# Attention and a gated long convolution: the fourth and fifth batch's last pair turned on TensorE, the last outputs reordered, and the order planned anew

## The chip, the cores and the metric

The kernel runs on one core of one Trainium2 chip. The metric is device time in microseconds (us). The kernel before took 386.67 us, the median of five runs (385.62 to 388.58).

A core has five engines that run side by side and wait for each other through semaphores: TensorE (PE: matrix products, and transposes against an identity matrix), ScalarE (ACT), VectorE (DVE), GpSimd (POOL) and SyncE (SP, which here only issues DMAs). Each engine works through its own list of instructions in order. TensorE writes to PSUM, which has eight banks. The rest lies in SBUF.

## The reference

There are 8 batches, 12 heads, 448 positions and 64 numbers per head. The first half is an attention with one extra term in the denominator; the second half projects its output three ways, convolves one of them cyclically along the sequence by means of a Fourier transform, multiplies the three and projects again.

```python
def _attn_ref(q, k, v):
    scale = 1.0 / np.sqrt(q.shape[-1])
    scores = scale * np.matmul(q, k.transpose(0, 1, 3, 2))
    m = np.max(scores, axis=-1, keepdims=True)
    e = np.exp(scores - m)
    attn = e / (np.sum(e, axis=-1, keepdims=True) + np.exp(-m) + 1e-09)
    return np.matmul(attn, v)

def _moe_ref(x, w_proj, filter_fft, w_out):      # x: (8, 448, 768), the heads side by side
    proj = x @ w_proj                            # w_proj: 768 x 2304
    x1, x2, x3 = proj[..., :D], proj[..., D:2 * D], proj[..., 2 * D:]
    X2 = np.fft.rfft(x2, n=S, axis=1)
    H = np.fft.rfft(filter_fft, n=S, axis=0)[None, :, :]
    x2_conv = np.fft.irfft(X2 * H, n=S, axis=1)
    return (x1 * x2_conv * x3) @ w_out
```

The kernel leaves out the subtraction of the maximum: dividing `exp(scores)` by its sum plus one is the same quotient.

## The kernel before

**Attention.** The heads go in pairs, six pairs to a batch, 48 in all (pair `i` belongs to batch `i // 6`; this document counts batches "first" to "eighth" in words, and from 0 in the code). For a pair, TensorE forms the scores (lines 773 and 775), ScalarE takes their exponential out of PSUM (780 and 786), TensorE multiplies them with v (798 and 806; the last column of v is one and gives the sum), and VectorE divides (819 to 821). The result lies in a tile `xb`, with positions down the partitions.

**From `xb` to `xT`.** The second half needs x with its 768 columns down the partitions, so each pair's `xb` is transposed into a tile `xT`. There are two ways. `x_dma` (line 892) lets SP issue one transposing DMA for several pairs; it is issued once after pair 2 of a batch, for pairs 0 to 2, and once for the rest. `x_pe` (line 901) makes four transposes on TensorE into a PSUM bank, and `x_back` copies them out (line 910 on VectorE, 908 on ScalarE). The first two batches use TensorE for all their pairs. The third batch uses DMA for pairs 0 to 4 and TensorE for pair 5. Which batches give pair 5 to the second DMA too is the constant `XALL`: before, the fourth to the eighth.

```python
if b in XALL or b > 1 and hp < NHP - 1:
    if hp in (2, NHP - 1 if b in XALL else NHP - 2):
        ps = range(0, 3) if hp == 2 else range(3, hp + 1)
```

**The second half**, `dense(b)`. VectorE folds `xT` (950 to 958). TensorE projects the fold, in the first four batches by blocks of frequencies (`P`, line 981), in the last four by columns (`PT`, line 1011), where the result, `x2T`, is turned by two transposing DMAs from SP (`rows_back`, line 1028). It is transformed (`Z`, 1049; copied by ScalarE at 1057), multiplied with the filter's spectrum (VectorE, 1063 and 1069), and transformed back (`I`, 1134, copied out at 1143, unfolded by VectorE at 1152 to 1163). The two other projections are the gates `G` (line 1095, six matmuls each, one for each of the six column blocks of `xT`); ScalarE copies the first (1107), VectorE multiplies it with the second (1110), and the product with the convolution at 1178. The output projection is `O` (line 1207): `st` 0 to 2 are the first three blocks of 128 positions, `st` 3 is the last 64 positions of two batches at once; each has two halves of 384 columns. ScalarE copies a half to a tile `osb` (1219, three buffers), and SP stores the 768 columns when both halves are there (1226, and 1229 for `st` 3).

**The last rows.** For the eighth batch the outputs came in the order `st` 0, 1, 3, 2, and `st` 2 had its own function `O_last` (line 1261 ff.): three pieces of 384, 192 and 192 columns, copied by ScalarE, ScalarE and VectorE into the free tile `nat` and stored by SP, ScalarE and SP, each as soon as it is copied.

**Loads.** In the first two batches q, k and v are cast and q and k turned on TensorE. From the third on, q comes by a casting load that GpSimd issues (536), k and v by SP's loads (585) that GpSimd casts (590 and 602), and q and k are turned by transposing DMAs from SP (542 and 547). The weights come by GpSimd's loads: `w_proj` in parts (751), the filter (667 ff.) and `w_out` (756).

**Who decides the order.** Every piece of work is a task with an engine, a planned cost, a due time, what it needs and makes, and which PSUM bank or buffer it takes and gives back. `Plan.run` runs through time on these costs: each engine that is free takes the ready task that is due first. The result is each engine's list of instructions; on the chip nothing is reordered. Due times come from the constants at the head of the kernel (`ATT`, `SLOT`, `DENSE`, `PACE`, `LEAD`, `LOAD` and others). For a DMA the planner adds 1.8 us and the task's own `late` to the transfer. PSUM banks are handed out by the same plan.

Of the kernel before, what the change touches and what calls it, by code (L numbers as in the profile page):

```python
# [19 lines left out]
D = H * DH  # L20
SP = 112
NST = S // SP
NDT = D // 128
NHP = H // 2
SCALE = 1.0 / float(np.sqrt(DH))
DCH = 384
# [15 lines left out]
class Plan:  # L42
# [26 lines left out]
    def add(self, eng, cost, want, emit, need=(), make=(), take=(), give=(), dma=0.0, run=256, n=1, after=0.0, begun=(), late=0.0):  # L69
        self.tasks.append((want, len(self.tasks), eng, cost, emit, need, make, take, give, dma, after, run, n, begun, late))  # L70
# [186 lines left out]
def kernel(  # L257
# [11 lines left out]
    nc = tc.nc  # L269
# [1 line left out]
    MAGIC = 12582912.0  # L271
    NSTAGED = 2
    SPIN = 38
    EARLY1 = 2.19
    ATT = [0.75, 24.41, 87.21, 101.61, 150.77, 186.69, 235.26, 286.49]
    SLOT = [2.52, 8.01, 4.27, 4.82, 6.44, 0.30, 6.71, 5.19]
    DENSE = [46.81, 84.00, 123.83, 169.80, 218.58, 253.46, 313.76, 296.92]
    PACE = [2.16, 2.30, 2.04, 2.28, 1.15, 2.55, 0.60, 1.33]
    FOLD = [-0.20, 0.45, -42.13, -39.60, 2.51, 0.15, -6.85, 0.77]
    BPS = 1.67  # L280
    RE1 = 22.20
    WT = 1.31
    FT = 21.96
    HALVED = (2,)
    AHEAD = [0, 0, 33.95, 43.62, 34, 34, 34, 34]
    LEAD = [-14.87, 8.62, 5.03, 10.66]
    LOADS = ((1, 0), (1, 1), ("F", None), (0, None), (2, None), ("O", None))
    LOAD = [22.29, 18.40, 18.46, 37.27, 38.16, 45.94]
    STEP = 2.26
    BYCOL = (4, 5, 6, 7)  # L290
    GLAST = 40.00
    XALL = (3, 4, 5, 6, 7)
    FOLD0 = (52.22, 39.65, 43.44)

    const = ctx.enter_context(tc.tile_pool(name="const", bufs=1))
    wts = ctx.enter_context(tc.tile_pool(name="wts", bufs=1))
# [16 lines left out]
    wout_bf = wts.tile([128, NDT, D], BF16, name="wout_bf")  # L313
# [8 lines left out]
    kT = [const.tile([128, NHP, 4, 128], BF16, name=f"kT{i}") for i in range(2)]  # L322
# [14 lines left out]
    nf = nat.bitcast(F32)  # L337
# [13 lines left out]
    add = plan.add  # L351
# [4 lines left out]
    def bank(hy):  # L356
        i = plan.banks[hy][0]
        return psum[:, 512 * i : 512 * i + 512]
# [167 lines left out]
    def loaded(b):  # L526
# [3 lines left out]
        parts = 2 if b in HALVED else 1  # L530
        size = NHP // parts
        few = 1 if b == NSTAGED else 3
# [20 lines left out]
        n = 0  # L553
        for part in range(parts):
            gs = slice(size * part, size * part + size)
            for st in range(NST):
                room = [("c" + w, i0 - 2) for w in "kqv"] if b == NSTAGED else [("qturn", b - 1, st)]
                add("POOL", 0.8 if parts > 1 else 0.95, want + STEP * n, lambda st=st, gs=gs: q_load(st, gs), need=room,
                    make=[("qn", b, part, st)], dma=1.3 / parts)
                n += 1  # L560
                add("SP", 1.3, want + 6.0 + STEP * n, lambda st=st, gs=gs: q_turn(st, gs), need=[("qn", b, part, st), last],
                    make=[("qturn", b, st)] + [("qT", i0 + i) for i in range(gs.start, gs.stop)], dma=0.6 / parts, late=0.7)

        for n, (name, x) in enumerate((("k", k), ("v", v))):
            add("SP", 0.5, tau(i0) - LEAD[0] - 0.2 + 0.1 * n,
                lambda name=name, x=x: nc.sync.dma_start(rests[:, "kv".index(name)], shared(x, b)),
                need=[("cr" + name, b - 1)], make=[("r" + name, b)], dma=1.05)
# [7 lines left out]
        for hp in range(NHP):  # L575
            g = i0 + hp
            for n, (name, x) in enumerate((("k", k), ("v", v))):
                slot = 2 * (g - NHP * NSTAGED) + n
                at = (KNAT + NST * D) // 2 + 384 * (slot % 5)
                src = nf[:, at : at + 384]  # L580
                old = slot - 5
                room = [("c" + "kv"[old % 2], NHP * NSTAGED + old // 2)] if old >= 0 else [
                    ("c" + w, i) for w in "kqv" for i in range(NHP * NSTAGED - 2, NHP * NSTAGED)]
                add("SP", 0.52, tau(g) - LEAD[0] + 0.1 * n,
                    lambda x=x, hp=hp, src=src: nc.sync.dma_start(src.rearrange("p (u c) -> p u c", u=2), rows(x, b, hp)),
                    need=room, make=[("s" + name, g)], dma=0.7, run=768)
                sv = src.rearrange("p (u j d) -> p u j d", u=2, j=3)
                if name == "k":
                    add("POOL", 0.6, tau(g) - LEAD[1],
                        lambda hp=hp, sv=sv: nc.gpsimd.tensor_copy(  # L590
                            kn[:, hp, 1:4].rearrange("p j (u d) -> p u j d", u=2), sv
                        ),
                        need=[("sk", g)] + (["zero kn"] if b == NSTAGED else [("kT", g - NHP)]), make=[("ck", g)])
                    if hp % few == 0:
                        gs = range(g, g + few)
                        add("SP", 1.3, tau(g) - LEAD[2], lambda hp=hp: k_turn(hp), need=[("ck", i) for i in gs] + [("crk", b), last],
                            make=[("kT", i) for i in gs], dma=0.6 * few, late=0.7)
                else:

                    def cast(hp=hp, sv=sv):  # L600
                        for u in range(2):
                            nc.gpsimd.tensor_copy(vn[b % 2][:, hp, 4 * u : 4 * u + 3, 0:DH], sv[:, u])  # L602

                    add("POOL", 0.72, tau(g) - LEAD[3], cast, need=[("sv", g), ("V", g - 2 * NHP, 1)], make=[("cv", g), ("v", g)])
# [104 lines left out]
    W = {}  # L709
# [51 lines left out]
    def attention(i):  # L761
# [153 lines left out]
        if b in XALL or b > 1 and hp < NHP - 1:  # L915
            if hp in (2, NHP - 1 if b in XALL else NHP - 2):
                ps = range(0, 3) if hp == 2 else range(3, hp + 1)
                add("SP", 1.3, w, x_dma, need=[("xb", NHP * b + h) for h in ps] + old,
                    make=[m for h in ps for m in (("X", NHP * b + h), ("xT", b, h))], dma=0.5 * len(ps), late=1.2)
        else:  # L920
            add("PE", 0.23, w, x_pe, need=[("xb", i)], make=[("X", i)], take=[("hy", ("X", i))])
            add("ACT" if on_act else "DVE", 0.43 if on_act else 0.33, w - 1.0, x_back, need=[("X", i)] + old, make=[("xT", b, hp)], give=[("hy", ("X", i))])


    def dense(b):
# [4 lines left out]
        def span(cost):  # L930

            w = DENSE[b] + at[0] * PACE[b]
            at[0] += cost
            return w
# [9 lines left out]
        def hold(key):  # L944
            return ("hy", key)
# [88 lines left out]
        def PT(dt):  # L1034
            hy = hold(("PT", b, dt))
            w = span(1.15)
            add("PE", 1.15, w, lambda: columns(dt, hy), need=[("xf", b, pg) for pg in range(4)] + [("w", 1, ch) for ch in range(2)],
                make=[("PT", b, dt)], take=[hy], give=[("xf", b)])
            add(("ACT", "DVE")[dt % 2], (0.43, 0.55)[dt % 2], w, lambda: columns_back(dt), need=[("PT", b, dt)],
                make=[("x2T", b, dt // 3)], give=[hy])  # L1040
            if dt % 3 == 2:
                ch = dt // 3
                add("SP", 1.3, w, lambda: rows_back(ch), need=[("x2T", b, ch)], make=[("x2", b, pg, ch) for pg in range(4)],
                    take=[("x2", b)], dma=1.5, late=1.2)

        def spectrum(pg, ch, hy):
            K = BLK_K[pg]
# [199 lines left out]
            if ch == 1:  # L1247
                add("SP", 0.6, w, lambda: store(st), need=[("os", b, st)], make=[("store", b, st)], give=[os_], dma=1.4, run=3072)

        def O_last(st):  # L1250
            rs = slice(st * 128, (st + 1) * 128)
            parts = ((0, DCH, "ACT"), (DCH, DCH // 2, "ACT"), (DCH + DCH // 2, DCH // 2, "DVE"))
            for n, (at, size, by) in enumerate(parts):
                hy = hold(("O", b, st, n))
                w = span(0.97 * size / DCH)
                c = slice(at, at + size)

                def product(hy=hy, c=c, size=size, n=n):
                    L["O", st, n] = bank(hy)
                    for dt in range(NDT):  # L1260
                        nc.tensor.matmul(
                            L["O", st, n][:, 0:size], W["yT", b][:, dt, rs], wout_bf[:, dt, c], start=(dt == 0), stop=(dt == NDT - 1)
                        )

                def back(size=size, c=c, n=n, by=by):
                    (nc.scalar.copy if by == "ACT" else nc.vector.tensor_copy)(nf[:, c], L["O", st, n][:, 0:size])

                def store_part(c=c, n=n):
                    (nc.scalar if n == 1 else nc.sync).dma_start(out[b, rs, c], nf[:, c])

                add("PE", 0.98 * size / DCH, w, product, need=[("y", b, 0), "wout"], make=[("O", b, st, n)], take=[hy],
                    give=[("yT", b)])
                add(by, (0.38, 0.25, 0.28)[n], w, back, need=[("O", b, st, n)], make=[("os", b, st, n)], give=[hy])
                add("ACT" if n == 1 else "SP", 0.6, w, store_part, need=[("os", b, st, n)], make=[("store", b, st, n)],
                    dma=1.4 * size / D, run=1536)

        if b and b + 1 < n_batches:
            G(0, 0), G(0, 1)
        if b in BYCOL and b + 1 == n_batches:
# [21 lines left out]
        for dt in range(NDT):  # L1301
            I(dt), G(2 + (dt + 1) // 2, (dt + 1) % 2)
        G(5, 1)
        for st in range(3) if b % 2 == 0 and b + 1 < n_batches else (0, 1, 3, 2) if b + 1 == n_batches else range(4):
            if (b, st) == (n_batches - 1, 2):
                O_last(st)
                continue
            for ch in range(2):
                O(st, ch)


    E = mybir.EngineType
# [103 lines left out]
```

## Time and profile before

| | |
|---|---|
| median of five runs | 386.67 us (385.62 to 388.58) |
| the profiled execution | 386.99 us |
| its span (first to last instruction on the core) | 384.9 us |
| TensorE, matmuls | 366.5 us, 95% of the span |
| TensorE, weight loads (beside matmuls) | 224.3 us, 58% |
| ScalarE | 261.2 us, 68% |
| VectorE | 259.2 us, 67% |
| GpSimd | 113.2 us, 29% |
| moved by DMA | 62.5 MB |

The profile is of one execution. Times in it are from the start of the span. A busy TensorE isn't TensorE at its peak: matmuls are pipelined, so the interval from one start to the next says more than the duration of one. `PEclk` is the clock that TensorE was granted, in tenths. A line of a timeline gives the start, the time, the engine, the line of the kernel, the operation, what it writes and reads and how often; the brackets at its end give how long the engine stood idle ahead of it, and for whom. `SPq` is SP's queue. In a list of waits the three numbers are the total, how often, and the longest.

### The profile page before, as it was taken

How to read it: one execution, taken by the hardware profiler on the slowest of the kernel's cores; microseconds unless marked ns; L12 is line 12 of the kernel's file. 1: busy time of each engine (PE TensorE's matmuls, PEld its weight loads, DVE VectorE, ACT ScalarE, POOL GpSimd, SP SyncE). 2: the span in 40 equal slices, each digit the busy share in tenths (PEclk: the TensorE clock that was granted, in tenths of full speed). 3: DMA queues.
4: the chain of work that ended last, by engine and by line, in shares of the span. 5: the costliest groups of instructions: out<-in, count | busy, mean ns of one | idle time of the engine just before them, and what ended most of it. 6: DMA issues, size and time to landing. Idle time of an engine off the chain costs nothing.

```text
span 384.9 us, 9526 instructions
## 1 busy us (share of the span) xinstructions
PE 366.5 (95%) x3678; PEld 224.3 (58%) x3678; DVE 259.2 (67%) x671; ACT 261.2 (68%) x456; POOL 113.2 (29%) x232
## 2 busy tenths in 40 slices
PE   8878999899999999969999999999999999999995
PEld 7546765566655676634675555555555655655553
DVE  7587579945789649647258974774369935982780
ACT  6777876666776878855688856685788757633633
POOL 5597383132464344614346350000000000000000
PEclk9999999999999999996999999999999999999999
DMA  8999999999999999999799996952241135045305
GB/s 205 242 249 242 241 211 214 133 99 281 192 215 213 129 277 233 207 162 274 182 255 158 197 254 116 176 143 84 75 93 21 22 84 122 3 84 122 125 0 165
DMA packets 149965, 62.53 MB, mean 162 GB/s; under 512 B 114525, under 2 KB 146464, under 8 KB 149920
## 3 DMA queue, kind: packets, MB, share of 16 engines
q1 hardware_dynamic: 112352, 52.05, 62.4%
q0 software_dynamic: 37184, 9.54, 26.7%
q8 instruction: 29, 0.48, 0.5%
q10 hardware_dynamic: 384, 0.33, 0.3%
q14 instruction: 16, 0.13, 0.1%
HBM read 43.86 MB, written 11.01 MB: 143 GB/s over the span
## 4 chain that ended last, share of the span: by engine, by line
PE 73%; DVE 14%; DMA 4%; issue 3%; ACT 3%; SPq 1%; POOL 1%; DVEq 0%; POOLq 0%; ACTq 0%
PE psum L1095 22%; PE psum L1207 13%; PE psum L806 8%; PE psum L981 7%; PE psum L773 7%; PE psum L1011 7%; DMA xT<-xb 2%; PE psum L1049 2%; DVE t L1063 2%; PE psum L775 2%; DVE xb L821 2%; PE psum L1134 2%; DMA nat<-in_q_dram 2%; DVE xf L958 1%; DVE cv L1163 1%
## 5 line engine op out<-in xcount | busy, mean ns | idle before, releaser
L780 ACT ACTIVATE e<-psum 128x896 bf16<-128x896 f32 x144 | 125.5, 923 | 23.2 <-PE psum L773 22.2
L1095 PE MATMUL psum<-xT,wproj_bf 128*128 128x448 bf16 x576 | 122.7, 356 | 4.6 <-DMA xT<-xb 3.5
L1095 PEld LDWEIGHTS <-wproj_bf 128*128 128x128 bf16 x576 | 54.6, 98 | 51.5 <-issue 8.8
L1207 PE MATMUL psum<-wout_bf,yT 128*128 128x384 bf16 x276 | 50.6, 326 | 0.0
L1107 ACT CAST x<-psum 128x448 bf16<-128x448 f32 x48 | 25.8, 537 | 30.0 <-PE psum L1095 23.7
L806 PE MATMUL psum<-vn,e 128*128 128x65 bf16 x1152 | 45.3, 195 | 0.0
L1219 ACT COPY osb<-psum 128x384 f32<-128x384 f32 x54 | 25.2, 483 | 23.7 <-PE psum L1207 23.3
L773 PE MATMUL psum<-qT,kT 64*128 64x448 bf16 x288 | 41.2, 358 | 0.0
L806 PEld LDWEIGHTS <-e 128*128 128x128 bf16 x1152 | 39.5, 98 | 2.6
L1063 DVE TENSOR_TENSOR t<-xs,hrs 113x768 bf16<-113x768 bf16 (+1 forms) x64 | 34.2, 573 | 8.5 <-ACT xs L1057 8.3
L602 POOL CAST vn<-nat 128x192 bf16<-128x192 f32 x72 | 27.4, 407 | 34.6 <-DMA nat<-in_v_dram 24.0
L819 DVE TENSOR_SCALAR rec<-psum 128x8 f32<-128x8 f32 x48 | 7.8, 161 | 43.6 <-PE psum L806 32.9
L1207 PEld LDWEIGHTS <-yT 128*128 128x128 bf16 x276 | 26.2, 97 | 18.3 <-issue 1.1
L1110 DVE TENSOR_TENSOR g<-x,psum 128x448 bf16<-128x448 bf16 x48 | 29.5, 616 | 9.4 <-PE psum L1095 7.3
L536 POOL DMA_DIRECT2D nat<-in_q_dram x28 | 24.8, 890 | 34.8 <-DMA qT<-nat 27.7
L981 PE MATMUL psum<-wproj_bf,xf 128*113 128x384 bf16 x192 | 35.0, 327 | 0.0
L821 DVE TENSOR_TENSOR xb<-psum,rec 128x512 bf16<-128x512 f32 x48 | 33.2, 691 | 1.7
L1011 PE MATMUL psum<-xf,wproj_bf 128*128 128x452 bf16 x144 | 30.4, 356 | 0.0
L1057 ACT CAST xs<-psum 113x384 bf16<-113x384 f32 (+1 forms) x64 | 27.5, 498 | 3.5 <-PE psum L1049 2.6
L786 ACT ACTIVATE er<-psum 128x448 bf16<-128x448 f32 x48 | 26.8, 558 | 4.5 <-PE psum L775 4.1
L1143 ACT CAST cr<-psum 128x452 bf16<-128x452 f32 x48 | 24.7, 555 | 6.4 <-PE psum L1134 6.4
L981 PEld LDWEIGHTS <-xf 128*113 128x113 bf16 x192 | 24.8, 132 | 6.8 <-issue 0.7
(117 smaller groups left out, 460.2 us busy)
## 6 DMA issues: line engine op xcount, KB each, us to landing
nat<-in_k_dram SPq DMA_DIRECT2D x48, 192.0 KB, 5.4
nat<-in_v_dram SPq DMA_DIRECT2D x48, 192.0 KB, 5.4
out_dram<-osb SPq DMA_DIRECT2D x23, 384.0 KB, 3.3
nat<-in_q_dram POOLq DMA_DIRECT2D x20, 168.0 KB, 7.9
nat<-in_q_dram SPq DMA_DIRECT2D x11, 224.0 KB, 6.8
wproj_bf<-in_moe_w_proj_dram POOLq DMA_DIRECT2D x2, 1152.0 KB, 16.6
rests<-in_k_dram SPq DMA_DIRECT2D x8, 192.0 KB, 5.3
rests<-in_v_dram SPq DMA_DIRECT2D x8, 192.0 KB, 7.0
```

Of the source, the lines that this page charges most:

```text
L602: nc.gpsimd.tensor_copy(vn[b % 2][:, hp, 4 * u : 4 * u + 3, 0:DH], sv[:, u])
L773: nc.tensor.matmul(sc[:, u, 0:S], kT[b % 2][c, hp, t, :], qT[b % 2][c, hp, :])
L780: nc.scalar.activation(e[:, 0 : 2 * S].rearrange("p (u n) -> p u n", u=2), pair(("sc", ("S", i, t)))[:, :, 0:S], AF.Exp, scale=SCALE,)
L806: nc.tensor.matmul(out_bank(u)[:, n, :], P["e"][1 + t][:, u * S + n * 128 : u * S + n * 128 + 128], vn[b % 2][:, hp, 4 * u + t, :], start= ...
L821: nc.vector.tensor_tensor(W["xb", b][:, hp].rearrange("p n (u d) -> p u n d", u=2), op[:, :, :, 0:DH], rec[:].unsqueeze(3).to_broadcast([1 ...
L981: nc.tensor.matmul(pps[:FQ, :DCH], W["xf", b][:, pg, kt, 0:FQ], wproj_bf[:, kt, D + ch * DCH : D + (ch + 1) * DCH], start=(kt == 0), stop= ...
L1011: nc.tensor.matmul(pps[:, 0 : 4 * FQ], wproj_bf[:, kt, D + dt * 128 : D + (dt + 1) * 128], W["xf", b][:, :, kt, 0:FQ], start=(kt == 0), st ...
L1057: nc.scalar.copy(L["xs", par, ch][:K, pg % 2, :], L["Z", pg, ch][:K, :DCH])
L1063: nc.vector.tensor_tensor(t[:K], L["xs", par, ch][:K], h, op=ALU.mult)
L1095: nc.tensor.matmul(p[:, :S], wproj_bf[:, kt, 2 * part * D + dt * 128 : 2 * part * D + (dt + 1) * 128], xT()[:, kt, 0:S], start=(kt == 0), ...
L1110: nc.vector.tensor_tensor(g[:, dt, :], L["x1", dt], p[:, :S], op=ALU.mult)
L1207: nc.tensor.matmul(ops[:n, :DCH], y[:, dt, 0:n], wout_bf[:, dt, ch * DCH : (ch + 1) * DCH], start=(dt == 0), stop=(dt == NDT - 1),)
```

## The change

It has three parts. `XALL` leaves out the fourth and fifth batch, so these turn pair 5 of x on TensorE as the third does, and their second transposing DMA takes pairs 3 and 4 alone. `O_last` is gone: the eighth batch's last rows go through `O` like all others, with ScalarE's copies and one store of 768 columns, and the outputs' halves come in another order. The planner is told that three kinds of transposing DMA land later (`late`), and its due times are others. The computation is the same.

```diff
-    EARLY1 = 2.19
-    ATT = [0.75, 24.41, 87.21, 101.61, 150.77, 186.69, 235.26, 286.49]
-    SLOT = [2.52, 8.01, 4.27, 4.82, 6.44, 0.30, 6.71, 5.19]
-    DENSE = [46.81, 84.00, 123.83, 169.80, 218.58, 253.46, 313.76, 296.92]
-    PACE = [2.16, 2.30, 2.04, 2.28, 1.15, 2.55, 0.60, 1.33]
-    FOLD = [-0.20, 0.45, -42.13, -39.60, 2.51, 0.15, -6.85, 0.77]
-    BPS = 1.67
-    RE1 = 22.20
+    EARLY1 = 5.03
+    ATT = [0.79, 17.21, 90.53, 105.41, 147.12, 188.78, 237.77, 285.73]
+    SLOT = [2.38, 8.68, 4.01, 3.23, 6.89, 0.31, 4.90, 5.05]
+    DENSE = [43.97, 82.34, 125.97, 170.34, 220.10, 253.73, 311.48, 304.06]
+    PACE = [1.76, 2.32, 1.55, 2.33, 1.19, 2.38, 0.76, 1.20]
+    FOLD = [-0.20, 0.39, -46.27, -39.52, 1.71, 0.19, -8.61, 0.59]
+    BPS = 1.80
+    RE1 = 13.75
...
-    FT = 21.96
+    FT = 20.85
...
-    AHEAD = [0, 0, 33.95, 43.62, 34, 34, 34, 34]
-    LEAD = [-14.87, 8.62, 5.03, 10.66]
+    AHEAD = [0, 0, 48.31, 45.28, 34, 34, 34, 34]
+    LEAD = [-24.87, 14.95, 5.88, 4.42]
...
-    LOAD = [22.29, 18.40, 18.46, 37.27, 38.16, 45.94]
-    STEP = 2.26
+    LOAD = [18.82, 18.41, 10.28, 37.96, 41.97, 46.86]
+    STEP = 1.79
...
-    XALL = (3, 4, 5, 6, 7)
-    FOLD0 = (52.22, 39.65, 43.44)
+    XALL = (5, 6, 7)
+    FOLD0 = (63.46, 45.82, 34.40)
...
                         add("SP", 1.3, tau(g) - LEAD[2], lambda hp=hp: k_turn(hp), need=[("ck", i) for i in gs] + [("crk", b), last],
-                            make=[("kT", i) for i in gs], dma=0.6 * few, late=0.7)
+                            make=[("kT", i) for i in gs], dma=0.6 * few, late=1.5)
...
                 add("SP", 1.3, w, x_dma, need=[("xb", NHP * b + h) for h in ps] + old,
-                    make=[m for h in ps for m in (("X", NHP * b + h), ("xT", b, h))], dma=0.5 * len(ps), late=1.2)
+                    make=[m for h in ps for m in (("X", NHP * b + h), ("xT", b, h))], dma=0.5 * len(ps), late=1.2 if b > 4 else 3.0)
...
                 add("SP", 1.3, w, lambda: rows_back(ch), need=[("x2T", b, ch)], make=[("x2", b, pg, ch) for pg in range(4)],
-                    take=[("x2", b)], dma=1.5, late=1.2)
+                    take=[("x2", b)], dma=1.5, late=2.5)
...
-        def O_last(st):
...
-        for st in range(3) if b % 2 == 0 and b + 1 < n_batches else (0, 1, 3, 2) if b + 1 == n_batches else range(4):
-            if (b, st) == (n_batches - 1, 2):
-                O_last(st)
-                continue
-            for ch in range(2):
+        if b + 1 == n_batches:
+            for st, ch in ((0, 0), (0, 1), (1, 0), (3, 0), (3, 1), (1, 1), (2, 0), (2, 1)):
                 O(st, ch)
+        else:
+            for st in range(3 + b % 2):
+                for ch in range(2):
+                    O(st, ch)
```

On each engine this gives another order of instructions, for the due times and the planned landings decide it.

More of the change, by code (lines that the diff above doesn't have):

```diff
@@ L1248, in O @@
                 add("SP", 0.6, w, lambda: store(st), need=[("os", b, st)], make=[("store", b, st)], give=[os_], dma=1.4, run=3072)
-        def O_last(st):
[L1251 to L1275, printed above, removed]
         if b and b + 1 < n_batches:
```

## The prediction

> **What bounds the kernel now.** I read the page first: who is busy, and where in the span TensorE is not.
>
> ```profile
> span 384.9 us, 9526 instructions
> PE 366.5 (95%) x3678; PEld 224.3 (58%) x3678; DVE 259.2 (67%) x671; ACT 261.2 (68%) x456; POOL 113.2 (29%) x232
> ...
> PE   8878999899999999969999999999999999999995
> ...
> PEclk9999999999999999996999999999999999999999
> ```
>
> TensorE is the bound: after its first 40 us it has one hole, in the slice of 173 to 183 us, where its clock falls too. TensorE's own list of waits names it:
>
> ```profile
> PE psum L901 <- DVE xb L821: 4.3, 3, 1.5
> PE psum L1095 <- DMA xT<-xb: 3.5, 1, 3.5
> ```
>
> The timelines of TensorE and of SP, and one line of the chain of waits, show the place:
>
> ```profile
> 167.70 0.35 PE L775 MATMUL psum<-qT,kT 128*128 128x448 bf16 x1
> 167.88 1.86 PE L1095 MATMUL psum<-xT,wproj_bf 128*128 128x448 bf16 x9
> 173.25 1.28 PE L1095 MATMUL psum<-xT,wproj_bf 128*128 128x448 bf16 x3 [3.50 <-DMA xT<-xb]
> 174.46 0.93 PE L773 MATMUL psum<-qT,kT 64*128 64x448 bf16 x4
> 175.18 0.43 PE L798 MATMUL psum<-vn,er 64*128 64x65 bf16 x8
> 175.54 1.50 PE L806 MATMUL psum<-vn,e 128*128 128x65 bf16 x24
> 176.85 2.43 PE L1095 MATMUL psum<-xT,wproj_bf 128*128 128x448 bf16 x6
> 179.07 0.52 PE L775 MATMUL psum<-qT,kT 128*128 128x448 bf16 x1
> 179.53 0.55 PE L773 MATMUL psum<-qT,kT 64*128 64x448 bf16 x4
> ```
>
> ```profile
> 162.69 1.58 SPq L542 DMA_TRANSPOSE qT<-nat  x1
> 164.72 4.39 SPq L892 DMA_TRANSPOSE xT<-xb  x1
> ```
>
> ```profile
> 164.72 8.48 DMA xT<-xb
> ```
>
> The gate products of the fourth batch (b = 3) have done three of six matmuls when they need x of pairs 3 to 5. That x was divided by 161.2, SP reached its transpose at 164.72, behind one of q, and it landed at 173.21. TensorE stood 3.50 us and then ran slow: 173.25 to 179.53 is 6.28 us for work that elsewhere takes 3.28 (half a gate 0.57, scores with rests 0.61, two value products 0.77, a gate 1.14, one score 0.19). The stop costs 3.50 + 3.00 = 6.5 us.
>
> **What the Trainium skill says.** "TensorE: Matmul & The Clock Gate", What's actually happening: a window of about 3.4 us without work halves TensorE's clock until it has been busy about as long. The trace agrees: 3.50 us idle, clock 0.79 over 168 to 176 us. "DMA: Bandwidth & Descriptors", Issuing engines are not separate DMA queues: transfers from SP, ScalarE and GpSimd share the same 16 engines. That fits: x transposes land in 3.3 to 10.0 us, median 3.9, the slow ones beside loads (DMA share 1.76 over 168 to 176).
>
> **The change, part by part.** I put the two programs' orders of TensorE work side by side and gave each piece its usual start-to-start time in this trace, so distances below are TensorE work.
>
> *X of the fourth and fifth batch.* The second DMA carries pairs 3 and 4 alone and starts from pair 4's value products. From there to the first gate it has 19.8 us (before 9.0, from pair 5's); in the fifth batch 18.1 (before 15.3). Pair 5 goes through TensorE: 13 us lie from its transposes to the gate. The slowest latency, 10.0, fits twice, less SP's queue. So the stop goes: -6.5. Added: eight transposes.
>
> ```profile
> L901 PE MATMUL psum<-ident_bf,xb x52: 217/219/230, 16.0 to 128.8; 128*128 128x128 bf16 x52
> ```
>
> Four start within 0.23 us (the matmul's 219 ns overlap), 2 x 0.23 = +0.46 on TensorE. The skill's Clock Gate page, Part 4: PE-mode transpose, prices one at 275 ns in context; at most 8 x 0.275 = 2.2 if nothing overlapped, and the trace decides. Two 0.38 us copies go to VectorE (67% busy), behind 13 us of other work. Each transpose stands 2.5 and 2.1 us after its pair's value products; third batch, 2.0, not stopped. SP issues as many transposes, two shorter; before the fifth batch's second stand two q transposes and four k and v loads whose buffers are free by then. Without that cover the wait is a new stop of the same kind.
>
> *The planner's times.* With transposes planned 0.8 to 1.8 us later, all is ordered anew. The first 44 us of TensorE work are the same but for neighbours swapped. The other handoffs over SP gain distance: third batch's second x 7.4 to 9.3, sixth 9.9 to 17.0, seventh 9.0 to 12.3; x2 at least 7.9 (before 6.9). The k of pairs 18 to 20 (landed 122.15, used 124.89, only 2.7 to spare) moves up: GpSimd casts pair 18's v ahead of the q load that held it for 5.1 us, so the k load that waits for that buffer goes out ahead of the x transpose and not behind, and SP reaches this k with one load fewer in between, by about 3 us. The k of pair 14 moves back behind two stores that end at 83; it landed at 87.4 and is used at 94.5, so the 2 to 3 us fit into 7. Stores that pass k and v loads cost SP 0.33 to 0.5 each, within the same distances.
>
> Second gain: at 58 us the scores of pair 9 take 1.33 instead of 0.61, a bank late from ScalarE; at 66 a gate takes 2.72 instead of 1.14, for the transpose behind it waits for `xb` 9, which stands on VectorE behind the whole fold of the second batch's first half. Now `xb` 9, pair 11's copies and pair 9's x come ahead of the fold; the transpose stands 1.6 us behind its value products and needs 0.2 + 1.05 + 0.2 plus what VectorE has left over. I leave 0.6 of the 2.3: -1.7 (0 to -2.3).
>
> Loss: some pieces move up to their bank's release: the first output of the third batch (1.57 us after the gate whose product frees the bank), a gate of the fourth, an output of the fifth (1.49), the sixth's second pair of outputs, the seventh's columns behind its fold. Each needs about 0.2 + 0.61 + 0.2 = 1.0 if VectorE is free, up to 0.8 more behind a division or product: 0 to 3, I take +0.8.
>
> *The end.*
>
> ```profile
> 378.53 2.13 PE L1261 MATMUL psum<-wout_bf,yT 128*128 128x384 bf16 x18
> ...
> 379.76 0.76 ACT L1266 COPY nat<-psum 128x384 f32<-128x384 f32 x2 [0.55 <-PE psum L1261]
> 380.44 1.12 SPq L1269 DMA_DIRECT2D out_dram<-nat  x2
> 380.55 0.37 ACTq L1269 DMA_DIRECT2D out_dram<-nat  x1
> 380.84 0.36 DVE L1266 COPY nat<-psum 128x192 f32<-128x192 f32 x1 [6.55 <-ACT nat L1266]
> ```
>
> The matmul time of the last rows is the same (0.98 against 2 x 0.49). The last copy is ScalarE's 0.48 of 384 columns for VectorE's 0.36 of 192: +0.12. The last store carries 384 KB: this trace's landed in 2.30 to 4.03 at the end, the last 96 KB in 2.66. The skill ("DMA: Bandwidth & Descriptors", Anatomy of one DMA) gives 2.0 us + bytes / 436 GB/s, so 2.9 and 2.2 by estimate, +0.7. I take 3.0 for 2.66. Its buffer is the first store's, issued 5 us before and landed in 2.3: free. +0.5 (0 to +1.6).
>
> **The sum.** -6.5 + 0.46 - 1.7 + 0.8 + 0.5 = -6.4. The profiled execution took 386.99 (span 384.93), 0.3 above the median of 386.67. 386.67 - 6.4 = 380.3 us.
>
> **Rivals.**
> *A wait comes back elsewhere* (0.14). Earlier TensorE meets the same loads sooner: pair 18's k had 2.7 us, and it is 2 us less if only TensorE moves; or one of the moved-up pieces stands behind VectorE and takes 3. 1.5 to 4.5 of the gain return: about 383. Against: that k's chain moves up as well.
> *The stop isn't typical* (0.08). It hangs on one transpose's 8.48 us; with 3.7, as in quiet stretches, it would have landed in time for none of it. Then only -1.7 + 0.46 + 0.8 + 0.5 remains: 386.7. Against: q's transpose issued beside it took 9.1, the traffic is the kernel's own, and five runs lie within 3 us.
> *VectorE becomes the bound* (0.03), in the stretches where it is 90% busy (60 to 80, 290 to 300): 385.
> *Slower: the third part of w_proj comes late* (0.05). Its load moves on GpSimd's queue behind three more casts, from 36.4 to about 41.4, where w_out's stood; its first user starts near 60. Before, the three big loads took 13.9, 19.3 and 21.2 us, but landed 7 us apart (48.5, 55.7, 62.6): they follow one another, and I expect 55.7 again. With 21.2 of its own it lands at 62.6 and costs 2.8. It decides against the change when it eats the 6.4, from 66.4 on; slower by 0.5% from 68.3, 27 us after issue: about 389. The longest load in the trace took 23.7.
>
> **Numbers.** Likeliest (0.70): 380.3, its own range 378.6 to 382.6, from the ends of the second gain, the moved-up pieces and the end. With the rivals, 8 in 10 lie between 378.7 and 384.6. 0.5% is 1.9 us, about what a measurement of this kernel can tell: faster means below 384.7, slower above 388.6. Faster takes the likeliest and nearly all of the first rival (0.84), same the untypical stop and VectorE (0.11), slower w_proj (0.05).
>
> **What would show it.** Right: TensorE's waits have no line for the fourth batch's `xT`, its clock stays full to the end, the fifth batch's gates follow without a hole; the wait of L901 on `xb` is below 3; w_proj's third part lands before 58; the last store is one of 384 KB, landing about 3 us after issue. Wrong: a wait of over 1 us of scores on `kT` or gates on `xT`, or on a bank from VectorE near the moved outputs, or a second clock dip.

## The result and the profile after

The kernel after takes 384.32 us (median of 43 runs, 382.16 to 389.29), the kernel before 386.54 (80 runs, 382.97 to 390.42). The ratio is 0.9952, with a 95% interval of 0.9937 to 0.9966: a gain of 1.9 us, between 1.3 and 2.4. The medians are of all runs and differ by 2.2; the ratio is of means and leaves out the slow runs of each kernel, those over 1.5% above its fastest. The forecast was 6.4.

The profiled execution of the kernel after took 386.62 us, 2.3 above its median. Its page, the same lines as before:

```profile
span 384.8 us, 9521 instructions
...
PE 368.5 (96%) x3681; PEld 226.0 (59%) x3681; DVE 258.8 (67%) x672; ACT 262.3 (68%) x456; POOL 113.6 (30%) x232
...
PE   8887999999999989999998999999999999999994
...
PEclk9998999999999989999999999999999999999998
```

The hole at 173 to 183 us is gone, and there is a new one in the slice of 135 to 144 us, where the clock falls too. TensorE's list of waits for the kernel after (total, how often, longest):

```profile
PE psum L901 <- DVE xb L821: 3.1, 3, 1.9
PE psum L773 <- ACT osb L1219: 1.8, 1, 1.8
...
PE psum L773 <- DVE xb L821: 1.0, 1, 1.0
```

No line is left for `xT`, and the transposes' wait on `xb` fell from 4.3 to 3.1. In their place scores (773) wait for ScalarE's copy of an output (1219). ScalarE's timeline, then TensorE's, then one piece of the chain of waits, all of the kernel after:

```profile
134.15 0.56 ACT L786 ACTIVATE er<-psum 128x448 bf16<-128x448 f32 x1
137.74 0.48 ACT L1219 COPY osb<-psum 128x384 f32<-128x384 f32 x1 [3.03 <-DMA out_dram<-osb]
138.11 0.48 ACT L998 CAST x<-psum 113x384 bf16<-113x384 f32 x1
138.48 1.75 ACT L780 ACTIVATE e<-psum 128x896 bf16<-128x896 f32 x2
```

```profile
135.89 0.55 PE L773 MATMUL psum<-qT,kT 64*128 64x448 bf16 x3
138.26 0.35 PE L773 MATMUL psum<-qT,kT 64*128 64x448 bf16 x1 [1.82 <-ACT osb L1219]
...
139.62 3.79 PE L981 MATMUL psum<-wproj_bf,xf 128*113 128x384 bf16 x12
```

```profile
131.22 6.49 DMA out_dram<-osb
```

ScalarE stands 3.03 us ahead of one copy into `osb`, and what ends its wait is a store. The output is the first half of `st` 3 of the first two batches. In units of TensorE work, it moved from 136.8 to 114.8, and the second half of `st` 2 just ahead of it from 134.7 to 113.1. So four output tiles now follow within about 8 us where there are three buffers, and the fourth has to wait until the first has been stored. The first tile was full at 123.9, but SP came to its store only at 131.22, behind the turning DMAs of k and q, and it landed 6.49 us later, at 137.71. The score that stands next on TensorE is released by the waiting copy itself, which frees a PSUM bank: it starts at 138.26, as the copy ends (137.74 + 0.48), and the exponentials behind the copy start later, at 138.48. TensorE stood for 1.82 us and soon after ran slow: twelve projections took 3.79 us, which take 2.11 at full clock.

To see where time went, I gave every piece of TensorE work its usual start-to-start time and added up, for stretches of the span, what it took beyond that. Microseconds above the usual:

| kernel | 0-40 | 40-80 | 80-120 | 120-160 | 160-220 | from 220 | all |
|---|---|---|---|---|---|---|---|
| before | 18.7 | 3.1 | 1.8 | 1.2 | 8.2 | 2.9 | 35.9 |
| before, again | 19.4 | 2.4 | 1.7 | 1.2 | 7.6 | 2.6 | 34.9 |
| before, 4 output buffers | 20.0 | 3.3 | 2.5 | 1.2 | 6.5 | 3.0 | 36.5 |
| before, part one alone | 18.9 | 2.4 | 2.0 | 1.3 | 4.2 | 2.4 | 31.2 |
| the same, again | 19.5 | 2.8 | 1.9 | 1.1 | 3.9 | 2.4 | 31.6 |
| after | 18.9 | 1.6 | 1.7 | 5.1 | 3.8 | 3.6 | 34.7 |
| after, again | 18.7 | 2.1 | 2.1 | 2.3 | 4.0 | 3.7 | 32.9 |
| after, 4 output buffers | 17.5 | 2.1 | 1.9 | 1.1 | 4.0 | 3.8 | 30.4 |
| the same, again | 19.2 | 2.0 | 2.0 | 1.2 | 3.9 | 3.6 | 31.9 |
| after, 4 buffers, no part one | 17.1 | 1.7 | 2.1 | 1.1 | 3.1 | 5.9 | 31.0 |

The first column is the start, where loads decide; it scatters by 1 us or so between executions of one kernel. The totals are good to about 1 us: the two traces of the kernel after differ by 1.8 here and by 2.8 in span.

### The profile page after: what moved, and what is told of

The parts are those of the page before. It is cut to its first block, busy times and chain, and to the rows that moved or that the text cites. A ratio compares the mean times of both kernels' runs of the same rounds, so it can differ in the third digit from the quotient of the medians.

```text
span 384.8 us, 9521 instructions
## 1 busy us (share of the span) xinstructions
PE 368.5 (96%) x3681; PEld 226.0 (59%) x3681; DVE 258.8 (67%) x672; ACT 262.3 (68%) x456; POOL 113.6 (30%) x232
## 4 chain that ended last, share of the span: by engine, by line
PE 75%; DVE 12%; DMA 4%; ACT 3%; issue 2%; SPq 2%; POOL 1%; ACTq 0%; POOLq 0%; DVEq 0%
PE psum L1095 24%; PE psum L1207 13%; PE psum L806 8%; PE psum L981 7%; PE psum L1011 7%; PE psum L773 7%; DMA out_dram<-osb 3%; DVE t L1063 2%; PE psum L1049 2%; PE psum L775 2%; DMA nat<-in_q_dram 2%; DVE yh L1069 2%; PE psum L1134 2%; PE psum L798 1%; DVE g L1110 1%
## 5 line engine op out<-in xcount | busy, mean ns | idle before, releaser
L1095 PE MATMUL psum<-xT,wproj_bf 128*128 128x448 bf16 x576 | 121.1, 352 | 1.3 <-DVE g L1110 1.1
L1207 PE MATMUL psum<-wout_bf,yT 128*128 128x384 bf16 x288 | 51.8, 326 | 0.2
L1219 ACT COPY osb<-psum 128x384 f32<-128x384 f32 x56 | 26.0, 484 | 29.2 <-PE psum L1207 24.4
L1063 DVE TENSOR_TENSOR t<-xs,hrs 113x768 bf16<-113x768 bf16 (+1 forms) x64 | 34.7, 577 | 9.5 <-ACT xs L1057 9.3
L602 POOL CAST vn<-nat 128x192 bf16<-128x192 f32 x72 | 28.3, 422 | 42.9 <-DMA nat<-in_v_dram 25.6
L1207 PEld LDWEIGHTS <-yT 128*128 128x128 bf16 x288 | 27.7, 98 | 19.4 <-issue 1.1
L981 PE MATMUL psum<-wproj_bf,xf 128*113 128x384 bf16 x192 | 36.8, 338 | 0.0
L590 POOL CAST nat<-nat 128x384 bf16<-128x384 f32 x36 | 20.7, 577 | 21.9 <-DMA nat<-in_k_dram 21.7
```

The lines of the kernel that those rows point to most:

```text
L981: nc.tensor.matmul(pps[:FQ, :DCH], W["xf", b][:, pg, kt, 0:FQ], wproj_bf[:, kt, D + ch * DCH : D + (ch + 1) * DCH], start=(kt == 0), stop= ...
L1063: nc.vector.tensor_tensor(t[:K], L["xs", par, ch][:K], h, op=ALU.mult)
L1095: nc.tensor.matmul(p[:, :S], wproj_bf[:, kt, 2 * part * D + dt * 128 : 2 * part * D + (dt + 1) * 128], xT()[:, kt, 0:S], start=(kt == 0), ...
L1207: nc.tensor.matmul(ops[:n, :DCH], y[:, dt, 0:n], wout_bf[:, dt, ch * DCH : (ch + 1) * DCH], start=(dt == 0), stop=(dt == NDT - 1),)
```

## The experiments

They were made in three groups, the kernels of a group in turn on one chip together with the kernel before. The medians of before in the three were 387.29, 385.99 and 385.63 us. Within a group its own times spread over 3.3 to 4.8 us, and the ratio of one kernel can differ between groups by 2 us while its medians agree (part one alone: 0.9861 and 0.9918, but 382.22 and 382.43).

**Is what the traces show typical?** Both kernels unchanged, once more.

> The changed kernel once more, for a second trace. Theory 1 (a new wait, for the third batch's output buffers: ScalarE's copy of an output stands until a store of three outputs earlier has landed, and scores wait behind it) expects the wait in this trace too, 1.5 to 3 us on ScalarE near 135 us, and 2 to 4 us of TensorE with it; ratio to before 0.993 to 0.997. Theory 2 (the stop on xT in the fourth batch, 6.5 us in the trace of before, is not typical of its executions) expects the ScalarE wait to be small or gone here, and the ratio near 0.995 all the same.

> The kernel before once more, for a second trace. Theory 1: the xT wait of the fourth batch is there again, over 2 us, with a dip of the clock. Theory 2: it is below 1 us or gone.

After: 384.11 us (383.59 to 389.78), ratio 0.9916 (0.9885 to 0.9946). Before, one run: 386.24, again with a stop of the gates on `xT`. TensorE's and ScalarE's lists of waits in the second trace of the kernel after:

```profile
PE psum L773 <- ACT osb L1219: 0.9, 1, 0.9
```

```profile
ACT osb L1219 <- DMA out_dram<-osb: 3.3, 2, 2.1
```

The new wait is there again but shorter: 0.9 us of TensorE for 1.82, with no slow clock behind it. The table has 2.3 for the stretch of 120 to 160 us where the first trace had 5.1 and the kernel before has 1.2. So the wait belongs to the kernel, and its size to the landing of one store. Of what was expected, the 2 us on ScalarE came, and the 2 to 4 us of TensorE did not in this trace.

**A fourth output buffer.** In the first experiment for the kernel after; the planner still counts three, so every engine's order stays as it is.

```diff
-    otp = ctx.enter_context(tc.tile_pool(name="otp", bufs=3))
+    otp = ctx.enter_context(tc.tile_pool(name="otp", bufs=4))
```

> The changed kernel with four buffers for the outputs instead of three; the planner still plans with three, so the order of all instructions is the same and only what the copies wait for changes. Theory 1: the wait near 135 us and the clock's dip behind it are gone, 2 to 4 us less than the changed kernel, ratio to before 0.985 to 0.990. Theory 2: the wait was one execution's; within 0.5 us of the changed kernel, ratio near 0.995.

> The kernel after with a fourth output buffer, once more, beside the same kernel with the old end, the same without part one, and part one alone, so that these four are compared directly. Theory (the fourth buffer leaves no further large wait): 381.5 to 382.5 us and narrow, ahead of the kernel before by 4 us or more; the line of osb on a landing store is absent from ScalarE's waits. Rival (what it gave was luck of the earlier call): 383.5 or more.

381.94 us (380.67 to 382.86), ratio 0.9856 (0.9827 to 0.9886); in the third group 382.33 (380.16 to 383.34), ratio 0.9906 (0.9876 to 0.9936). Beside the unchanged kernel after, in the same group, that is 2.2 us less (resampling the two sets of runs gives 0.9 to 5.9). ScalarE's and TensorE's timelines with four buffers:

```profile
133.25 0.51 ACT L1219 COPY osb<-psum 128x384 f32<-128x384 f32 x1
```

```profile
134.58 0.55 PE L773 MATMUL psum<-qT,kT 64*128 64x448 bf16 x4
...
136.14 2.11 PE L981 MATMUL psum<-wproj_bf,xf 128*113 128x384 bf16 x12
```

The copy starts at once, the four scores run through, and the twelve projections take 2.11. Nothing but the buffer was changed, so the wait on the stores is the cause, and its price in usual runs is about 2 us.

**The same buffer in the kernel before.**

> The kernel before with a fourth output buffer and nothing else; every engine has the same order. Theory (the wait for an output buffer is new in the kernel after, because the third output of the second batch and that of the second and third batch moved up by 20 us of TensorE work): no change, ratio 0.999 to 1.001. Rival (a fourth buffer helps any order of this kernel, so that what it gave the kernel after is not the price of the change): 0.994 to 0.996.

386.84 us (382.92 to 390.77, 20 runs), ratio 1.0006 (0.9982 to 1.003): nothing. The kernel before has no use for it, so what it gives the kernel after is a price of the new order. The trace served for something else too. TensorE's timeline at the stop:

```profile
174.84 0.96 PE L1095 MATMUL psum<-xT,wproj_bf 128*128 128x448 bf16 x3 [2.66 <-DMA xT<-xb]
```

The stop was 2.66 us here, not 3.50, mostly because the transpose landed in 7.76 us and not in 8.48 (in the second trace of before it was 4.1). With the slow clock behind it, 160 to 180 us took 4.9 above the usual, against 6.9 in the first trace; without a stop it is about 0.5.

**Part one alone**, in the kernel before.

```diff
-    XALL = (3, 4, 5, 6, 7)
+    XALL = (5, 6, 7)
```

> The kernel before with the first part of the change alone (XALL without the fourth and fifth batch; due times, planned landings and last outputs as before), which inserts the two groups of transposes and leaves nearly all the order of TensorE. Theory 1 takes the stop of the trace as typical: 5 to 6.5 us less than before, ratio 0.983 to 0.987. Theory 2: 0 to 2.5 us less, ratio 0.994 to 1.000.

> The kernel before with XALL = (5, 6, 7) alone. Theory (part one alone takes the whole stop): 381.8 to 382.5 us, 4 to 5 below the kernel before and within 0.5 of the kernel after with four buffers, so the new due times bring nothing beside it. Rival (the new order is worth the 1 us that was counted for the stretch from 58 to 70 us): 1 us slower than the kernel with the fourth buffer.

382.22 us (381.76 to 382.5), ratio 0.9861 (0.9836 to 0.9886); in the third group 382.43 (381.09 to 385.47), ratio 0.9918 (0.9891 to 0.9945). In both traces the wait on `xT` is gone: the transpose of pairs 3 and 4 landed at 162.79 in the first, and the first gate started at 168.98. Over 18 runs the median is 382.4, 4.2 below the kernel before (5.1 and 3.2 in the two groups), and level with the kernel after and four buffers (382.2 over 16 runs; the difference is 0.1, from -0.6 to 1.0). The new due times, planned landings and end together bring nothing that shows beside part one.

The table says why 4.2 and not 6. From 160 to 220 us the kernel before stands 6.5 to 8.2 above the usual, part one alone 3.9 and 4.2. Without the stop's 4.4 to 6.4 some 2 should have been left. The other 2 are new waits at 180 to 220 us, where the lists of the first two traces of the kernel before are empty. With part one alone TensorE's list for that stretch begins so:

```profile
PE psum L1207 <- DVE xb L821: 0.6, 1, 0.6
PE psum L1049 <- DVE x L996: 0.5, 1, 0.5
PE psum L1095 <- DVE xT L910: 0.4, 1, 0.4
```

The kernel after, whose order is another, loses as much there. TensorE's timeline shows its largest wait, and the last 20 us by windows (engine after engine, busy us in 20) come from the kernel before, from the kernel after and from part one alone:

```profile
204.38 0.36 PE L773 MATMUL psum<-qT,kT 64*128 64x448 bf16 x2 [0.95 <-DVE xb L821]
```

```profile
200.00:220.00 20.00, 20.00 (x212) 11.67 (x211) 17.97 (x49) 16.62 (x30) 8.27 (x13) 1.00 1.36 183
```

```profile
200.00:220.00 20.00, 18.30 (x202) 10.42 (x199) 19.52 (x51) 15.66 (x26) 10.79 (x18) 1.00 1.40 210
```

```profile
200.00:220.00 20.00, 19.34 (x207) 11.10 (x206) 16.54 (x45) 15.08 (x26) 9.64 (x17) 1.00 1.49 197
```

The third number after the length is VectorE. In this trace of the kernel after it is busy for 19.52 of 20 us, but it needn't be full for the loss: with part one alone it has 16.54, with four buffers 16.12 and 17.06, and what is lost from 160 to 220 us is the same 4 us. TensorE waits for single results that come late from VectorE. Why they are late here and not in the kernel before was not tried.

**The new order without part one**, with four buffers so that the store's wait doesn't hide the answer.

```diff
-    XALL = (5, 6, 7)
+    XALL = (3, 4, 5, 6, 7)
```

> The kernel after with a fourth output buffer, and with XALL as it was before, (3, 4, 5, 6, 7): so the new due times and later planned landings alone, without the transposes of part one on TensorE. In this order the first gate of the fourth batch stands 15.3 us of TensorE work behind what releases its transposing DMA, in place of 9.0 before; 13.9 in the fifth batch, 8.3 in the seventh, 9.1 in the eighth. Theory A (part one took the stop away, the order alone does not): a wait of gates on xT of 2 us or more comes back and the ratio lies near 0.992 to 1.0. Theory B (later planned landings alone give the transfer the time it needs, and part one was not needed beside them): no line of gates on xT in the fourth batch, and eight transposes less on TensorE, so 0.46 us less than the kernel after with four buffers: 0.984 to 0.985. With 8.3 and 9.1 us left, a wait on xT in the seventh or eighth batch would be a third outcome, at 0.986 to 0.99.

> The kernel after with a fourth output buffer and without part one (XALL as before). Theory (the new order alone stretched the transfer's distance enough; part one adds eight transposes and nothing else): no wait of gates on xT in the fourth batch, and a time within 0.6 us of the kernel with the fourth buffer, on its lower side. Rival (without part one a wait comes in some executions): its slowest runs reach 384 or more and the median is 1 us higher.

382.98 us (381.34 to 383.74), ratio 0.9922 (0.9898 to 0.9946); again 382.65 (380.45 to 385.32), ratio 0.9915 (0.9879 to 0.9952). TensorE's lists name no wait of gates on `xT` in either. SP's timeline of the first, and then TensorE's:

```profile
164.63 3.67 SPq L892 DMA_TRANSPOSE xT<-xb  x1
```

```profile
174.58 1.48 PE L1095 MATMUL psum<-xT,wproj_bf 128*128 128x448 bf16 x6
```

This transpose took 10.66 us and landed at 175.29. The gate had started at 174.58, and its fourth matmul, the first to need it, would come 0.57 later, at 175.14. It started at 175.33, just after the landing: a wait of 0.19, too short for the list. In the second trace the transpose landed at 174.79, and the gate started at 176.08. So the new due times and later planned landings alone would have taken the stop away, but only just; part one leaves 11 us (164.07 to 175.31, in the first trace with four buffers). In time the two can't be told apart: without part one +0.3 in the third group (-1.1 to +1.4; its slowest run took 385.32, the slowest with part one 383.34), where eight transposes less should give -0.46. That those cost 0.46 is thus neither shown nor contradicted.

**The end alone.** First the old end (`O_last`, old order of the last outputs) put back into the kernel after with four buffers, then the new end put into part one alone.

```diff
-        if b + 1 == n_batches:
-            for st, ch in ((0, 0), (0, 1), (1, 0), (3, 0), (3, 1), (1, 1), (2, 0), (2, 1)):
-                O(st, ch)
...
+        for st in range(3) if b % 2 == 0 and b + 1 < n_batches else (0, 1, 3, 2) if b + 1 == n_batches else range(4):
+            if (b, st) == (n_batches - 1, 2):
+                O_last(st)
+                continue
```

> The kernel after with a fourth output buffer, and with the last rows as they were before (the function O_last and the order st 0, 1, 3, 2). Everything up to the last outputs is in the same order as with the fourth buffer alone. Theory (the new end costs, as the traces read: 1.66 us from the last landing to the end of the span in place of 1.04, and the last copy 0.1 later): TensorE's end to the end of the span falls from about 4.8 us to 4.3, and the time from 381.9 to 381.4, ratio 0.984 to 0.985. Rival (the difference at the end is only scatter of the last landing and of GpSimd's last instructions): no difference, 0.9856. Second rival (the three short stores are the slower ones): 0.987.

> The same with the last rows as they were before. Theory (the end costs 0.1 to 0.2 us, as the first pair of traces now reads: 4.7 us from TensorE's end to the end of the span against 4.8): no difference that can be measured from the kernel with the fourth buffer alone, within 0.5 us. Rival (the new end costs 0.5 us or more): 0.5 to 1 us faster than the kernel with the fourth buffer alone.

> The kernel before with XALL = (5, 6, 7) and with the changed end (no O_last, the halves in the new order, one store of 768 columns), and nothing else; the due times and the planned landings are those of before. With XALL alone the ratio was 0.9861. Theory (the new end costs 0.5 us): 0.9874, about 382.7 us, and TensorE's end to the end of the span is about 4.8 us in place of 4.2. Rival (the end costs nothing): 0.986.

Old end: 382.63 us (381.69 to 383.05) and 381.41 (380.85 to 382.42); ratios 0.992 (0.99 to 0.9941) and 0.9888 (0.9851 to 0.9925). Beside the new end in the same group it was 0.9 less, with an interval from 0.4 more to 1.9 less: unclear. New end on part one: 382.2 (381.48 to 383.55), ratio 0.9914 (0.9892 to 0.9937), against 382.22 and 382.43 without it. The traces are sharper. From TensorE's end to the end of the span:

| | old end | new end |
|---|---|---|
| old order | 4.28, 4.29, 4.28, 4.26, 4.26 | 4.37 |
| new order | 4.72, 4.73 | 4.83, 4.82, 4.81, 4.80; without part one 4.96, 4.66 |

The new end costs 0.1. The other 0.4 goes with the new order whatever the end is. It comes after the last landing (1.04 us from there to the end of the span before, 1.49 with the old end in the new order, 1.62 after). My theory that the new end costs 0.5 falls; what the 0.4 is has stayed open.

The kernel after's end, from TensorE's, SP's and ScalarE's timelines:

```profile
376.84 3.09 PE L1207 MATMUL psum<-wout_bf,yT 128*128 128x384 bf16 x18
...
378.75 2.36 SPq L1226 DMA_DIRECT2D out_dram<-osb  x2
379.89 0.86 ACT L1219 COPY osb<-psum 128x384 f32<-128x384 f32 x2 [1.40 <-DMA out_dram<-osb]
```

The last store is issued at 380.78 and lands at 383.14: 2.36 us for 384 KB.

**The best version.** The kernel after with a fourth output buffer and part one alone both beat both kernels, at 382.2 and 382.4 us. Between them, and the others without a large wait, these runs don't decide.

## Why the prediction was wrong

*The stop goes.* The mechanism was right: no wait on `xT`, and part one alone removes it. Its worth was not. -6.5 took one profiled execution's stop as usual and its full price as gain. Other executions of the kernel before paid 4.4 to 6.1, and about 2 us came back at 180 to 220 us. Net, 160 to 220 us went from 7.4 (mean of three) to 4.0. This term was -3.4 (-4.3 by the count at the end of this section). The sum had no term for waits that come back behind the stop: it had waits on VectorE only where pieces move up, and VectorE as the bound (0.03) in other stretches. What came back are waits for single results of VectorE, with VectorE busy for 16.1 to 19.5 of the last 20 us; why they came back is open.

*The stores.* This is the step that failed outright: "Stores that pass k and v loads cost SP 0.33 to 0.5 each, within the same distances". I counted a store as time on SP, not as the release of one of three output buffers. For the pieces that move up I went through the PSUM banks that they take, and not through the tile that their copy goes into. The list of moved pieces even lacks the two outputs that move by 22 us. The wait that came cost 1.1 us in one trace and 3.9 in another (120 to 160 us, 2.3 and 5.1 against 1.2), and about 2 in the medians. The rival that comes nearest is the first, "a wait comes back elsewhere" (0.14, about 383), but at a place which that rival didn't name. The sign given for it, a second clock dip, is what the page shows.

*The second gain*, -1.7: 40 to 80 us went from 2.9 (mean of three) to 1.6 and 2.1, so about -1.1. The score's wait at 58 us is gone. The gate at 66 still loses 0.6, now to the product `g`.

*The moved-up pieces*, +0.8: from 220 us on it is 3.6 and 3.7 against 2.8, so +0.9, apart from the stores above. The size fits by luck: TensorE's lists of waits from 220 us on are empty in both traces of the kernel after, and these lists go down to 0.2 us, so it is not made of pieces that wait for their banks.

*The end*, +0.5: 0.55 came, by luck, for it came at another place. The last 384 KB landed in 2.36 us, not in 3.0, and from TensorE's end to the last landing nothing changed (3.24 before, 3.22 after). "Its buffer is the first store's [...]: free" was wrong too: that store took 4.47 us and ScalarE waited 1.40 for it, so that the last copy ended 0.83 after TensorE and not 0.52 as with four buffers. The last landing came no later for it (3.20 with four buffers). Nearly all of the 0.55 comes after the last landing.

*`w_proj`'s third part* landed at 56.2, for the 55.7 expected; that rival fell.

With the second trace of the kernel after, the terms of the table are -3.4 (stop) - 0.8 (40 to 80, 2.1 for 2.9) + 1.1 (stores) + 0.1 (80 to 120) + 0.9 (from 220) - 0.7 (start, 18.7 for 19.4, scatter) + 0.46 (transposes, as estimated) + 0.55 (end) = -1.8. That this is near the measured -1.9 is luck: the span of this trace is 3.1 shorter than the mean of the three of before (381.9 for 385.0). A count by single matmuls, each against the median start-to-start time of its kind in all traces, does add up to that: -4.3 (160 to 220), -0.8 (40 to 80), +1.0 (120 to 160), +0.5 (80 to 120), +0.5 (from 220), -0.9 (start), +0.3 (matmuls added and gone) and +0.55 (end). The medians differ by less than these executions, so the shares in the missing 4.5 us are rough: 2.2 to 3.1 lie in the stop's size and what followed it, 1 to 2 in the output buffers and 0.6 to 0.9 in the second gain; the start, which scatters, gave 0.7 to 0.9 back here.

## What to carry to other kernels

The price of a stop is the most that its removal can give: look at how long it is in several executions, and expect small waits to come back just behind it. When work moves earlier, go through everything that it takes, output buffers as well as banks, and take the time after which each comes back from transfers in the same stretch, not in a quiet one. Where a planner decides the order, compare its landing times with the traces: this store was planned to land 3.2 us after its issue at the earliest (1.4 and 1.8) and took 6.49, and the copy that waited for it stood ahead of work that could have run. A longer landing in the plan, or an earlier place for the store on SP, was not tried.

## What the runs showed of the hardware

The same 384 KB store landed in 2.36 to 2.66 us at the end of the span, as the last, and in 6.49, 6.97 and 7.47 us between 131 and 141 us, beside loads and turning DMAs. The estimate of 2.9 us that I had from the Trainium skill ("DMA: Bandwidth & Descriptors", Anatomy of one DMA) is near the first and far from the second. That section gives its numbers for DMAs that GpSimd issues; these are issued by SP, which the prediction passed over.

TensorE's clock fell after less idle time than the prediction's text has from "TensorE: Matmul & The Clock Gate", What's actually happening (about 3.4 us). Even in the first trace of before, which the prediction reads as agreeing, the stop began at 169.75 and the clock was at half from 172.6 to 179.4: it fell 2.8 us into the stop. It fell after 2.66 us in the kernel before with four buffers, and after 1.82 us in the kernel after, but there only when work had run again for over 1 us: 1.00 from 139.0 to 139.6, 0.50 from 139.7 to 143.1. After 0.9 us in its second trace it didn't fall. The length of the stop alone doesn't decide: at 30 us the kernel after and the same with four buffers both stood for 1.92 us between the same pieces of work; in the first the clock was at 0.50 from 33.9 to 37.2, in the second at 1.00 from 30 to 38. What else decides wasn't tried.

The fourth batch's second transposing DMA of x took 3.1 to 4.9 us when it was issued at 159 to 164 us for two pairs, and 7.8 to 10.7 when it was issued at 164.6 to 167.0 for three. With four buffers, 5 us less to the issue made 11 less to the landing (with part one and without). Whether the number of pairs or the traffic at that time makes the difference, these runs don't separate.
